# Feed-forward stage: order of PSUM copies around a late narrow product, and two banks for the first narrow products

## The chip, the cores and the metric

The kernel runs on one core of a Trainium2 chip. The metric is device time in microseconds of one execution. Engines: TensorE (PE; its weight loads are PEld), VectorE (DVE), ScalarE (ACT), GpSimd (POOL) and SyncE (SP, which issues the DMAs). PE results land in PSUM, eight banks of 512 fp32 words per partition; ACT and DVE read them from there.

## What is computed

Three layers run one after the other on 4 x 768 tokens (8 heads of 48, so 384 features). Only the last one is touched; the second one hands it its input as a product of two thin matrices.

```
y   = linear_attention(r, k, v, w, u)        # 3072 x 384
c   = softmax(y @ phi, axis=1)               # 3072 x 32
x   = c @ slot_out                           # 3072 x 384, slot_out is 32 x 384
h   = x @ w_in                               # 3072 x 2048
g   = where(h > 0, h, exp(min(h, 0)) - 1)
out = g @ w_out                              # 3072 x 384
```

The weights w_in and w_out arrive as 64-bit floats; the kernel reads them as pairs of 32-bit words and turns them into fp32 itself.

## The kernel before

**The feed-forward by narrow products.** Because x is c @ slot_out, the kernel never forms x. It forms slot_out @ w_in (32 x 2048, the *narrow products*) and then h transposed, block by block, from it and from c transposed. Each fp32 factor of a wide matmul is carried as a rounded part (*high*, written by ACT as fp32r) and the rest (*low*, written by DVE as the difference), side by side in the partitions. So a narrow product must go PE -> PSUM -> ACT `high` -> DVE `low` before a wide matmul can use it as a weight. `through` (L1125) makes the product for 2n columns: two halves `a` of n columns each, the first on partitions 0 to 63 of a PSUM tile `phm`, the second on partitions 64 to 127; the matmuls of the halves alternate over three steps of the contraction. `high` (L1139) and `low` (L1142) round one half into `mst`.

**PSUM.** The pool `fh_p` has two tiles of two banks each, for h (`ph[n]`, "fh" in the profile). The pool `fo_p` has four tiles of one bank, tag `fo`, given out in turn: to the narrow products, and then to the output sums `po[blk, t]`, four for each block of 512 tokens (t = 0 to 3). A tile that is given out again can be written only when the last reader of its previous holder is done.

**Start of the stage.** Columns 0 to 255 (m0) and 256 to 511 (m1) are made first, L1149, each in one `fo` tile, and rounded in the order high(0), low(0), high(1), low(1). Then `hid(0)` (h of the first unit: two matmuls, the first needs half 0 of m0, the second half 1), then the products m3 (columns 1024 to 1279) and m2 (512 to 1023) on PE, while ACT and DVE begin the activation of unit 0 (`tanh`, `expo` on ACT; `neg`, `elu` on DVE; `upper`, the high part of g, on ACT; `lower`, its low part, on DVE). ACT has the roundings of m3 and m2 in between these.

**The main loop.** A unit n is one block of 512 tokens with two tiles of 128 hidden columns; there are 48: first, for each of the six blocks, the five pairs among the first ten column tiles (units 0 to 29; unit n is of block n // 5), then the three pairs of the last six. Step n of the loop issues `hid(n)` on PE; on ACT `leave` (copies of finished sums), `tanh(n)`, `leave`, `expo(n)`, `upper(n-1)`; on DVE `neg(n)`, `lower(n-1)`, `elu(n)`; then, on PE, the output products `outp(n-3, (2, 3))` and `outp(n-2, (0, 1))`, 24 matmuls in all (L1261, L1262, L1264). Steps 6 to 31 without 12 and 22 also carry the widening of late weights (ACT, DVE, POOL, and DMAs on SP), and steps 26, 30 and 33 split late weights (L1286, L1287).

**Sums.** When the fifth pair of a block has been added, the sums of its four `po` tiles are put on the list `done`. `leave(k)` takes k of them off and has ACT copy each to `acc` (L1198). A block's sums 0 and 1 join the list at the end of one step, and 2 and 3 during the next.

**The late product.** At step 22 (`PAUSE[1]`), after `outp(19, (2, 3))`, the kernel makes the narrow product of the columns 1280 to 2047 (`columns(CA, CB // 2)`, "m" below), and rounds it: high(0), low(0), high(1), low(1). The columns are used from unit 30 on. This product takes one `fo` tile between the four of block 3 and the four of block 4. So it takes the bank of block 3's sum 0, and block 4's sums 0, 1, 2 take those of block 3's sums 1, 2, 3, and block 4's sum 3 that of the late product. Block 3's sums 0 and 1 are copied in step 22 itself, its sums 2 and 3 at the top of step 23 on ACT, behind the roundings of the late product. On PE, `outp(20, (0, 1))` of step 22 comes right behind the late product and opens block 4's sums 0 and 1.

```
            if n == PAUSE[1]:
                m = columns(CA, CB // 2)
                for i in range(2):
                    high(*m, i)
                    low(*m, i)
            if n - 2 < N:
                outp(n - 2, (0, 1))
```

The order on each engine is the order of the text; waits between the engines follow from the tiles.

Of the kernel before, what the change touches and what calls it, by code (L numbers as in the profile page):

```python
# [8 lines left out]
F32 = mybir.dt.float32  # L9
# [4 lines left out]
ALU = mybir.AluOpType  # L14
# [222 lines left out]
def kernel(  # L237
# [14 lines left out]
    nc = tc.nc  # L252
# [43 lines left out]
    for a in range(2):  # L296
# [5 lines left out]
        out=mask, in_=mask, compare_op=ALU.is_gt, fill=0.0, base=0, pattern=[[1, 128]], channel_multiplier=-1  # L302
# [94 lines left out]
    with ExitStack() as actx:  # L397
# [333 lines left out]
        def part(j):  # L731
            fs = [[logits], [slots_a], [], [slots_b], [slots_c], [slots_d], [slots_e], [slots_f], []]
            fs = [[(f, j) for f in l] for l in fs]

            def stage(l):
                for f, i in l:
                    f(i)

            return [lambda l=l: stage(l) for l in fs]
# [208 lines left out]
    def half(name, dtype=F32):  # L948
        return ht_p.tile([128, 1024], dtype, tag="ht", name=name)
# [36 lines left out]
    for a in range(2):  # L986
        for q in range(4):
# [3 lines left out]
                out=s3, in_=s3, compare_op=ALU.is_ge, fill=0.0, base=-spe * e, pattern=[[1, NS]],  # L991
# [3 lines left out]
                out=s3, in_=s3, compare_op=ALU.is_ge, fill=0.0, base=spe * e + spe - 1, pattern=[[-1, NS]],  # L995
# [107 lines left out]
    sT = mid.tile([128, KD, 64], F32, name="sT")  # L1103
# [12 lines left out]
    fo_p = main.enter_context(tc.tile_pool(name="fo_p", bufs=4, space=PSUM))  # L1116
# [5 lines left out]

    mst = [half(f"mst{i}", F32R) for i in range(2)]

    def through(c, n, ph):  # L1125
        src, c0 = (win, 0) if c < CA else (win2, CA)
        for kk in range(KD):
            for a in range(2):
                nc.tensor.matmul(
                    out=ph[64 * a:64 * a + 64, :n], lhsT=sT[:, kk, :],  # L1130
                    rhs=src[:, kk, c - c0 + n * a:c - c0 + n * a + n], start=(kk == 0), stop=(kk == KD - 1),
                )
        return ph, c, n

    def halves_of(c, n, a):
        o = mst[c // 1024][:, c % 1024 + n * a:c % 1024 + n * a + n]
        return o[64 * a:64 * a + 64], o[64 - 64 * a:128 - 64 * a]

    def high(ph, c, n, a):  # L1139
        nc.scalar.copy(out=halves_of(c, n, a)[0], in_=ph[64 * a:64 * a + 64, :n])  # L1140

    def low(ph, c, n, a):  # L1142
        hi, lo = halves_of(c, n, a)
        nc.vector.tensor_tensor(out=lo, in0=ph[64 * a:64 * a + 64, :n], in1=hi.bitcast(F32), op=ALU.subtract)  # L1144

    def columns(c, n):
        return through(c, n, fo_p.tile([128, 512], F32, tag="fo", name="phm"))

    m0, m1 = columns(0, 128), columns(256, 128)  # L1149
    for m in (m0, m1):  # L1150
        for i in range(2):
            high(*m, i)
            low(*m, i)
# [19 lines left out]
    def late_wide(j, f):  # L1173
        if 0 <= j < NPB:
            raw, a, dst = pieces[j]
            if f is wide_d:
                f(raw, a, dst)
                del pieces[j]
                if j + 2 < NPB:
                    late_load(j + 2)  # L1180
            else:
                f(raw, a)
# [9 lines left out]
    def leave(n=1):  # L1192
        for _ in range(n):
            if done:
                o, r, second = done.pop(0)
                a = acc[r // 8][:, r % 8, :]
                if not second:
                    nc.scalar.copy(out=a, in_=o)  # L1198
                    continue
                if r < NT // 128 - 4:  # L1200
                    os_ = f2.tile([128, DM], F32, tag="os", name="os", bufs=4)
                    nc.scalar.copy(out=os_, in_=o)  # L1202
                    nc.gpsimd.tensor_tensor(out=a, in0=os_, in1=a, op=ALU.add)  # L1203
                else:
                    nc.vector.tensor_tensor(out=a, in0=o, in1=a, op=ALU.add)
                nc.sync.dma_start(out=out[128 * r:128 * r + 128, :], in_=a)


    ph, th, ex = {}, {}, {}
    NARROW, HALF = 4, 6  # L1210

    def hid(n):
        blk, f = units[n]
        ph[n] = fh_p.tile([128, 2, TB], F32, tag="fh", name="fh")
        for i in range(2):
            nc.tensor.matmul(  # L1216
                out=ph[n][:, i, :], lhsT=mst[(f + i) // 8][:, 128 * ((f + i) % 8):128 * ((f + i) % 8) + 128],
                rhs=cT[:, TB * blk:TB * blk + TB], start=True, stop=True,
            )
        th[n] = f2.tile([128, 2, TB], F32, tag="th", name="th")  # L1220
        ex[n] = f2.tile([128, 2, TB], F32, tag="ex", name="ex")
# [7 lines left out]
    def neg(n, s):  # L1229
        nc.vector.scalar_tensor_tensor(  # L1230
            out=ex[n][:, s], in0=ex[n][:, s], scalar=1.0, in1=th[n][:, s], op0=ALU.add, op1=ALU.mult
        )

    def elu(n, s):
        nc.vector.scalar_tensor_tensor(  # L1235
            out=ex[n][:, s], in0=ex[n][:, s], scalar=0.0, in1=ph[n][:, s], op0=ALU.min, op1=ALU.max
        )
# [7 lines left out]
    def lower(n, s):  # L1245
        nc.vector.tensor_tensor(  # L1246
            out=gl[n][:, s], in0=ex[n][:, s], in1=gh[n][:, s].bitcast(F32), op=ALU.subtract
        )
# [19 lines left out]
    def outp(n, ts):  # L1268
        for t in ts:
            for i in range(2):  # L1270
                term(n, i, t, (0, 1))
        if TB // 128 - 1 in ts:
            gh.pop(n), gl.pop(n)

    def outp_first(n, done=()):
        for x in range(2):
            for i in range(2):
                for t in range(TB // 128):
                    if (i, t, x) not in done:
                        term(n, i, t, (x,))  # L1280
        gh.pop(n), gl.pop(n)

    def late_split(f):
        a, b = (t[:, f % 8:f % 8 + 2, :] for t in whl[f // 8])
        w = wo2[:, f - FA:f - FA + 2, :]
        nc.scalar.copy(out=a, in_=w)  # L1286
        nc.vector.tensor_tensor(out=b, in0=w, in1=a.bitcast(F32), op=ALU.subtract)  # L1287

    def both(f, n, s=slice(0, 2)):
        if 0 <= n < N:  # L1290
            f(n, s)
# [5 lines left out]
    def narrow(n):  # L1297
        u = n - 1
        neg(u, ta)
        lower(u - 1, tb)  # L1300
        elu(u, ta)
        tanh(n, ta)
        upper(u, ta)
        neg(u, tb)
        expo(n, ta)
        lower(u, ta)
        elu(u, tb)
        tanh(n, tb)
        upper(u, tb)
        expo(n, tb)  # L1310
# [7 lines left out]
    tanh(0, ta)  # L1318
    expo(0, ta)
    high(*m3, 0)  # L1320
    tanh(0, tb)
    expo(0, tb)
    high(*m3, 1)
    neg(0, ta)
    elu(0, ta)
# [8 lines left out]
    for i in range(2):  # L1334
        low(*m3, i)
    lower(0, ta)
    elu(0, tb)
    for i in range(2):
        low(*m2, i)
# [8 lines left out]
    for n in range(2, N + 3):  # L1348
        if n < N:
            hid(n)  # L1350
        if n <= NARROW:
            narrow(n)
        else:
            if n == NARROW + 1:
                neg(n - 1, slice(0, 2))
                lower(n - 2, tb)
                elu(n - 1, slice(0, 2))
            leave(1 if done and done[0][1] % 4 == 0 else 2)
            both(tanh, n)
            leave()  # L1360
            both(expo, n)
            both(upper, n - 1)
            j, h = divmod(steps.index(n), 2) if n in steps else (-1, 0)
            if h == 0:
                late_wide(j, wide_a)
            if n in SPLIT:
                late_split(FA + 2 * SPLIT.index(n))
            both(neg, n)
            both(lower, n - 1)
            both(elu, n)  # L1370
            for f in (wide_b3, wide_c, wide_d) if h else (wide_b1, wide_b2):
                late_wide(j, f)
        if n < HALF:
            outp_first(n - 2, early if n == 2 else ())
        else:
            if n > HALF:
                outp(n - 3, (2, 3))
            if n == PAUSE[1]:
                m = columns(CA, CB // 2)
                for i in range(2):  # L1380
                    high(*m, i)
                    low(*m, i)
            if n - 2 < N:
                outp(n - 2, (0, 1))
    leave(4)
# [36 lines left out]
```

## Time and profile before

| | us |
|---|---|
| three runs | 454.84, 455.89, 456.1 |
| median | 455.89 |
| profiled execution, its own time | 454.1 |
| profiled execution, span from first to last instruction | 452.4 |
| PE busy in it | 414.1 (92%) |
| DVE busy in it | 369.3 (82%) |
| ACT busy in it | 262.2 (58%) |
| mean granted TensorE clock | 0.995 |

Times in the rows count from the start of the span. A timeline row has the start, the length, engine, line, operation, and in brackets how long the engine had stood idle before it and what ended that. The length of a matmul runs to its modelled end, so in a stream the matmuls overlap and the distance of their starts is what one costs. The feed-forward stage runs from about 202 us to the end.

### The profile page before, as it was taken

The page shows a single profiled execution, that of the slowest core. Times are in us where ns is not written, and L with a number is a line of the kernel's source. Part 1 is how long each engine was busy: PE and PEld are TensorE (multiplying, and loading weights), DVE is VectorE, ACT ScalarE, POOL GpSimd, SP SyncE. Part 2 cuts the span into 40 slices and gives each one's busy share as a digit, 9 for nine tenths or more (in the row PEclk, how much of TensorE's full clock was granted, in tenths as well). Part 3 has the DMA queues.
Part 4 walks back from the last instruction along what each step waited for, and adds up shares of the span by engine and source line. Part 5 has one row for each costly group of instructions (what it writes and reads, how often), then busy time and mean ns, then how long its engine had stood idle before and what let it go on. Part 6 is the DMA issues. An engine that isn't in the chain of part 4 may idle for free.

```text
span 452.4 us, 10086 instructions
## 1 busy us (share of the span) xinstructions
PE 414.1 (92%) x4021; PEld 361.4 (80%) x4021; DVE 369.3 (82%) x581; ACT 262.2 (58%) x482; POOL 157.2 (35%) x170
## 2 busy tenths in 40 slices
PE   6988988898988989997999999998999899999995
PEld 5876776776776874455999999996989889999994
DVE  5899989899898744768889999995989889768661
ACT  2543453545453332337787878874777768776750
POOL 2355455456446413500003333350213135423340
PEclk9999999999999999999999999998999999999999
DMA  8979799999999968940001111111111002011212
GB/s 124 227 163 268 191 258 265 266 282 186 269 266 260 278 212 280 313 175 1 0 1 35 36 35 38 35 36 35 36 35 35 1 0 72 35 54 52 71 71 76
DMA packets 97575, 57.41 MB, mean 127 GB/s; under 512 B 77808, under 2 KB 89328, under 8 KB 97520
## 3 DMA queue, kind: packets, MB, share of 16 engines
q1 hardware_dynamic: 96704, 56.64, 46.0%
q8 instruction: 33, 0.54, 0.5%
q14 instruction: 22, 0.18, 0.1%
q10 hardware_dynamic: 816, 0.05, 0.1%
HBM read 51.96 MB, written 4.72 MB: 125 GB/s over the span
## 4 chain that ended last, share of the span: by engine, by line
PE 54%; DVE 24%; issue 9%; ACT 7%; DMA 3%; SPq 1%; POOL 1%; DVEq 0%; ACTq 0%; POOLq 0%
PE fo L1261 10%; PE fo L1264 10%; PE fo L1262 10%; DVE ex L1235 4%; DVE ex L1230 4%; PE fh L1216 3%; PE py L612 3%; PE ps_k L522 3%; PE ps_a L554 2%; PE pd L1029 2%; PE ph L1007 2%; DVE am L559 2%; PE py L625 2%; DVE km L517 2%; DVE scr L317 2%
## 5 line engine op out<-in xcount | busy, mean ns | idle before, releaser
L1261 PE MATMUL fo<-wh,gh 128*128 128x384 f32 x384 | 130.8, 341 | 3.8 <-ACT acc L1198 2.7
L1262 PE MATMUL fo<-wl,gh 128*128 128x384 f32 x384 | 130.1, 339 | 0.0
L1264 PE MATMUL fo<-wh,gl 128*128 128x384 f32 x384 | 125.9, 340 | 3.3 <-DVE gl L1246 3.3
L1230 DVE SCALAR_TENSOR_TENSOR ex<-ex,th 128x1024 f32<-128x1024 f32 (+1 forms) x52 | 60.9, 1172 | 23.8 <-ACT ex L1227 23.6
L1261 PEld LDWEIGHTS fo<-wh,gh 128*128 128x128 f32 x384 | 72.5, 189 | 8.6 <-ACT acc L1198 4.3
L1264 PEld LDWEIGHTS fo<-wh,gl 128*128 128x128 f32 x384 | 72.0, 188 | 4.2 <-DVE gl L1246 4.2
L1262 PEld LDWEIGHTS fo<-wl,gh 128*128 128x128 f32 x384 | 72.4, 189 | 1.9
L1224 ACT ACTIVATE th<-fh 128x1024 f32<-128x1024 f32 (+1 forms) x53 | 50.4, 951 | 38.0 <-PE fh L1216 38.0
L1246 DVE TENSOR_TENSOR gl<-ex,gh 128x1024 fp32r<-128x1024 f32 (+1 forms) x52 | 68.3, 1314 | 1.7 <-ACT gh L1243 1.3
L336 POOL TENSOR_TENSOR cv<-raw,cv 128x384 f32<-128x384 f32 x12 | 19.4, 1620 | 136.5 <-ACT gh L1243 51.5
L1235 DVE SCALAR_TENSOR_TENSOR ex<-ex,fh 128x1024 f32<-128x1024 f32 (+1 forms) x52 | 58.8, 1131 | 0.5 <-ACT ex L1227 0.4
L1227 ACT ACTIVATE ex<-fh 128x1024 f32<-128x1024 f32 (+1 forms) x53 | 50.3, 949 | 9.7 <-DVE gl L1246 9.5
L1243 ACT CAST gh<-ex 128x1024 fp32r<-128x1024 f32 (+1 forms) x52 | 51.4, 988 | 6.2 <-DVE ex L1235 4.9
L1203 POOL TENSOR_TENSOR acc<-os,acc 128x384 f32<-128x384 f32 x20 | 26.7, 1346 | 44.0 <-ACT os L1202 44.0
L646 ACT COPY xT<-ps_x 128x384 f32<-128x384 f32 x24 | 11.5, 479 | 43.2 <-PE ps_x L644 43.2
L583 POOL TENSOR_TENSOR qc<-t,w 128x192 f32<-128x192 f32 x20 | 14.5, 725 | 59.7 <-DVE t L582 21.8
L1216 PE MATMUL fh<-cT,mst 128*128 128x512 f32 x96 | 31.1, 404 | 1.9 <-DVE mst L1144 1.1
L559 DVE TENSOR_TENSOR am<-ps_a,mask 128x512 f32<-128x512 f32 x48 | 30.7, 678 | 0.2 <-PE ps_a L554 0.2
L529 DVE TENSOR_TENSOR qd<-rT,ps_k 128x512 f32<-128x512 f32 x24 | 16.5, 686 | 15.3 <-ACT kT L527 15.3
L554 PE MATMUL ps_a<-rT,kT 64*128 64x128 f32 x384 | 27.9, 285 | 0.3 <-ACT kT L527 0.2
L522 PE MATMUL ps_k<-ident,km 128*128 128x128 f32 x96 | 15.6, 285 | 12.4 <-ACT xT L646 6.4
L625 PE MATMUL py<-vd,am 128*64 128x48 f32 x768 | 26.5, 222 | 0.0
(161 smaller groups left out, 695.0 us busy)
## 6 DMA issues: line engine op xcount, KB each, us to landing
we<-in_moe_w_dram SPq DMA_DIRECT2D x14, 768.0 KB, 8.0
we<-in_moe_w_dram SPq DMA_DIRECT2D x16, 512.0 KB, 6.2
rp<-in_r_dram SPq DMA_DIRECT2D x24, 192.0 KB, 4.6
rk<-in_k_dram SPq DMA_DIRECT2D x24, 192.0 KB, 4.6
vd<-in_v_dram SPq DMA_DIRECT2D x24, 192.0 KB, 4.8
out_dram<-acc SPq DMA_DIRECT2D x24, 192.0 KB, 1.9
we<-in_moe_w_dram SPq DMA_DIRECT2D x16, 256.0 KB, 5.4
scr<-in_moe_w_out_dram SPq DMA_DIRECT2D x10, 384.0 KB, 5.7
```

The costliest lines, as they stand in the source:

```text
L554: nc.tensor.matmul(out=aps[a][:, p, :], lhsT=kT[q, p, :], rhs=rT[n][q, p, :], start=True, stop=True)
L559: nc.vector.tensor_tensor(out=am[n, a], in0=aps[a], in1=mask.unsqueeze(1).to_broadcast([128, HP, 128]), op=ALU.mult)
L1216: nc.tensor.matmul(out=ph[n][:, i, :], lhsT=mst[(f + i) // 8][:, 128 * ((f + i) % 8):128 * ((f + i) % 8) + 128], rhs=cT[:, TB * blk:TB * b ...
L1224: nc.scalar.activation(out=th[n][:, s], in_=ph[n][:, s], func=ACTF.Tanh, scale=0.5)
L1227: nc.scalar.activation(out=ex[n][:, s], in_=ph[n][:, s], func=ACTF.Exp)
L1230: nc.vector.scalar_tensor_tensor(out=ex[n][:, s], in0=ex[n][:, s], scalar=1.0, in1=th[n][:, s], op0=ALU.add, op1=ALU.mult)
L1235: nc.vector.scalar_tensor_tensor(out=ex[n][:, s], in0=ex[n][:, s], scalar=0.0, in1=ph[n][:, s], op0=ALU.min, op1=ALU.max)
L1243: nc.scalar.copy(out=gh[n][:, s], in_=ex[n][:, s])
L1246: nc.vector.tensor_tensor(out=gl[n][:, s], in0=ex[n][:, s], in1=gh[n][:, s].bitcast(F32), op=ALU.subtract)
L1261: nc.tensor.matmul(out=o, lhsT=gh[n][:, i, s], rhs=wh, start=(f == first), stop=False)
L1262: nc.tensor.matmul(out=o, lhsT=gh[n][:, i, s], rhs=wl, start=False, stop=False)
L1264: nc.tensor.matmul(out=o, lhsT=gl[n][:, i, s], rhs=wh, start=False, stop=(f == final))
```

## The change

Three things. The first two narrow products get a list of two `fo` tiles each, one for each half (`part` picks the tile). At step 22 `leave(2)` is put in front of the late product. And the late product's two roundings are issued before its two low parts.

```diff
+    def part(ph, n, a):
+        return (ph[a] if isinstance(ph, list) else ph)[64 * a:64 * a + 64, :n]
+
     def through(c, n, ph):
...
-                    out=ph[64 * a:64 * a + 64, :n], lhsT=sT[:, kk, :],
+                    out=part(ph, n, a), lhsT=sT[:, kk, :],
...
     def high(ph, c, n, a):
-        nc.scalar.copy(out=halves_of(c, n, a)[0], in_=ph[64 * a:64 * a + 64, :n])
+        nc.scalar.copy(out=halves_of(c, n, a)[0], in_=part(ph, n, a))
...
-        nc.vector.tensor_tensor(out=lo, in0=ph[64 * a:64 * a + 64, :n], in1=hi.bitcast(F32), op=ALU.subtract)
+        nc.vector.tensor_tensor(out=lo, in0=part(ph, n, a), in1=hi.bitcast(F32), op=ALU.subtract)
...
-    m0, m1 = columns(0, 128), columns(256, 128)
+    m0 = through(0, 128, [fo_p.tile([128, 512], F32, tag="fo", name=f"phm{i}") for i in range(2)])
+    m1 = through(256, 128, [fo_p.tile([128, 512], F32, tag="fo", name=f"phm{i}") for i in range(2)])
...
             if n == PAUSE[1]:
+                leave(2)
                 m = columns(CA, CB // 2)
-                for i in range(2):
-                    high(*m, i)
-                    low(*m, i)
+                for f in (high, low):
+                    for i in range(2):
+                        f(*m, i)
```

## Rows read from the trace of the kernel before

**Rows 1.** Page, busy tenths and granted clock in 40 slices of 11.3 us.

```profile
PE   6988988898988989997999999998999899999995
DVE  5899989899898744768889999995989889768661
PEclk9999999999999999999999999998999999999999
```

**Rows 2.** Windows: us, busy time and count by engine, clock, DMA.

```profile
234.60:281.00 46.40, 45.95 (x255) 44.64 (x254) 44.90 (x50) 36.41 (x48) 15.32 (x8) 1.00 0.12 35
281.00:299.00 18.00, 18.00 (x101) 17.46 (x100) 17.38 (x20) 14.57 (x19) 6.73 (x4) 1.00 0.12 36
308.17:312.00 3.83, 1.63 (x10) 1.00 (x6) 3.26 (x4) 1.46 (x4) 0.00 (x0) 0.94 0.09 35
312.00:316.00 4.00, 3.98 (x14) 3.79 (x15) 0.06 (x1) 1.18 (x2) 0.00 (x0) 0.63 0.00 0
330.00:373.00 43.00, 39.94 (x218) 37.90 (x216) 37.04 (x41) 32.33 (x42) 11.73 (x8) 1.00 0.06 19
373.00:447.00 74.00, 73.50 (x408) 72.02 (x408) 54.44 (x49) 48.77 (x62) 26.68 (x20) 1.00 0.17 60
```

**Rows 3.** Timeline of PE around the late product (L1129) and the first halted sum.

```profile
299.04 0.62 PE L1216 MATMUL fh<-cT,mst 128*128 128x512 f32 x2
303.72 0.62 PE L1216 MATMUL fh<-cT,mst 128*128 128x512 f32 x2
304.18 0.34 PE L1261 MATMUL fo<-wh,gh 128*128 128x384 f32 x1
306.12 0.34 PE L1264 MATMUL fo<-wh,gl 128*128 128x384 f32 x1
306.39 2.16 PE L1129 MATMUL phm<-win,sT 128*64 128x384 f32 x12
308.47 0.44 PE L1261 MATMUL fo<-wh,gh 128*128 128x384 f32 x1
309.46 0.34 PE L1264 MATMUL fo<-wh,gl 128*128 128x384 f32 x1
312.02 0.69 PE L1261 MATMUL fo<-wh,gh 128*128 128x384 f32 x1 [2.23 <-ACT acc L1198]
314.11 1.03 PE L1216 MATMUL fh<-cT,mst 128*128 128x512 f32 x2
319.19 0.63 PE L1216 MATMUL fh<-cT,mst 128*128 128x512 f32 x2
```

**Rows 4.** Timeline of ACT, step 22 and the start of step 23.

```profile
304.38 1.03 ACT L1224 ACTIVATE th<-fh 128x1024 f32<-128x1024 f32 x1 [0.55 <-PE fh L1216]
306.58 1.05 ACT L1243 CAST gh<-ex 128x1024 fp32r<-128x1024 f32 x1
308.62 0.47 ACT L1140 CAST mst<-phm 64x384 fp32r<-64x384 f32 x1 [0.98 <-PE phm L1129]
310.99 0.47 ACT L1140 CAST mst<-phm 64x384 fp32r<-64x384 f32 x1 [1.90 <-DVE mst L1144]
311.49 0.86 ACT L1198 COPY acc<-fo 128x384 f32<-128x384 f32 x2
315.18 1.03 ACT L1224 ACTIVATE th<-fh 128x1024 f32<-128x1024 f32 x1 [2.82 <-PE fh L1216]
```

**Rows 5.** Timeline of DVE over the same steps.

```profile
309.16 1.21 DVE L1235 SCALAR_TENSOR_TENSOR ex<-ex,fh 128x1024 f32<-128x1024 f32 x1
310.41 0.55 DVE L1144 TENSOR_TENSOR mst<-phm,mst 64x384 fp32r<-64x384 f32 x1
317.15 1.23 DVE L1230 SCALAR_TENSOR_TENSOR ex<-ex,th 128x1024 f32<-128x1024 f32 x1 [5.09 <-ACT ex L1227]
```

**Rows 6.** Timeline of the stage's start: roundings, low parts and unit 0.

```profile
202.25 1.53 PE L1129 MATMUL phm<-win,sT 128*64 128x128 f32 x24 [0.32 <-DVE sT L1105]
203.51 0.28 DVE L1144 TENSOR_TENSOR mst<-phm,mst 64x128 fp32r<-64x128 f32 x1 [1.31 <-ACT mst L1140]
203.83 0.55 ACT L1140 CAST mst<-phm 64x128 fp32r<-64x128 f32 x2 [0.35 <-DVE mst L1144]
204.47 0.19 PEld L1216 LDWEIGHTS fh<-cT,mst 128*128 128x128 f32 x1 [0.43 <-DVE mst L1144]
204.77 0.26 ACT L1140 CAST mst<-phm 64x128 fp32r<-64x128 f32 x1 [0.39 <-DVE mst L1144]
204.90 2.17 PE L1129 MATMUL phm<-win,sT 128*64 128x128 f32 x24
205.05 0.60 ACT L1224 ACTIVATE th<-fh 128x512 f32<-128x512 f32 x1
215.71 0.70 PE L1216 MATMUL fh<-cT,mst 128*128 128x512 f32 x2 [0.67 <-DVE ex L1235]
```

**Rows 7.** Other halts of PE in the main loop (timeline of PE).

```profile
238.25 0.44 PE L1261 MATMUL fo<-wh,gh 128*128 128x384 f32 x1 [0.45 <-ACT acc L1198]
337.33 0.44 PE L1264 MATMUL fo<-wh,gl 128*128 128x384 f32 x1 [0.99 <-DVE gl L1246]
357.94 0.44 PE L1264 MATMUL fo<-wh,gl 128*128 128x384 f32 x1 [1.23 <-DVE gl L1246]
```

## What the change should do to the time

> **What bounds the kernel now.** I read the slices first: PE is busy at nine tenths almost throughout from 202 us on, DVE close behind it, and the granted clock shows one slice below nine, the 28th, from 305 to 317 us [rows 1]. Then the windows of the stage: PE has 18.00 us of work in 18.00 us before the late product and 73.50 in 74.00 at the end; between 330 and 373 us it loses some 3 us to DVE, 39.94 of 43.00; and between 308 and 316 us it loses more in 8 us than anywhere else, first standing still (1.63 busy of 3.83), then at a mean clock of 0.63 [rows 2]. So outside a few places the end of the kernel is the start of the stage plus PE's work plus PE's halts, and a halt that goes is worth its length unless something later re-creates it. The change touches the start of the stage and the one long halt. The timelines of these two places carry the rest.
>
> **Part 1, the copies in front of the late product.** PE takes 4.68 us for a unit (hid at 299.04 and 303.72), 0.46 of it for hid (the next matmul starts at 304.18) and 4.22 / 24 = 0.176 for each output matmul [rows 3]. In step 22 it makes the late product from 306.39 to 308.47, adds to block 4's sum 0 until 309.64 (last start 309.46 plus 0.176), and then stands until 312.02, where the wait for ACT's copy L1198 ends [rows 3]. That copy starts at 311.49, right behind the second rounding at 310.99, which itself waited 1.90 us for DVE's first low part; that one could start only at 310.41, when DVE had finished `elu` of 309.16 [rows 4, 5]. So PE waits for a copy whose data have been there since 306.5 (the matmul of 306.12 plus its 0.34 [rows 3]) and which is queued on ACT behind a rounding that waits for DVE.
>
> With the change ACT has the two copies behind `upper` of 306.58, which takes 1.05 us: they start by 307.65 and, at 0.86 for the two, are done by 308.5 [rows 4]. PE wants sum 1's bank at 309.64, so there is 1.1 us to spare. ACT meets the late product at 308.62 as before and rounds both halves by 309.6, before DVE is free at 310.4; DVE's low parts then follow back to back, 310.41 to 311.5 [rows 4, 5]. No transfer moves with the copies: L1198 issues no DMA in the first half of the stage, and no instruction of POOL or SP is passed.
>
> The worth: PE's halt from 309.64 to 312.02 is 2.38 us. The six matmuls of sum 1 then take 312.02 to 314.11, 2.09 us where six in a stream take 6 x 0.176 = 1.06, so 1.03 more; and hid(23) to hid(24) takes 319.19 - 314.11 = 5.08 us in place of 4.68, 0.40 more [rows 3]. The last two are the clock: granted at 0.63 on average between 312 and 316 us, after the halt, which is a part at the lower level of 1.2 GHz [rows 2]. A halt of 1.23 us later on is in a window whose clock is 1.00 [rows 2, 7], so the fall goes with the long halt, and I count it as removed. Sum 2.38 + 1.03 + 0.40 = 3.8 us. Bounds: 2.4 if the clock still falls; 3.9 if the slower first matmul after the product goes too.
>
> What is late next? hid(23) comes at 309.64 + 1.06 = 310.7, tanh(23) 0.66 later at 311.4 (303.72 to 304.38 in step 22), where ACT is free since 309.6 [rows 3, 4]. Then `expo`, and DVE's `neg(23)` two ACT instructions after tanh, 1.97 us as from 315.18 to 317.15, so at 313.3 [rows 4, 5]. DVE is free at 311.5: of its idle 5.09 us about 1.8 remain, so it is not behind and step 23 starts for PE, ACT and DVE in the same relation as before, only 3.8 us earlier. Block 4's sum 3 takes the late product's bank: PE wants it after hid(23) (0.46) and six matmuls, at 310.7 + 0.46 + 1.06 = 312.2, and DVE has read it at 311.5; 0.7 us to spare.
>
> Everything after is tied to step 23 by waits among the same engines, the halts for DVE between 330 and 373 us too; these should come 3.8 us earlier and be as long.
>
> **Part 2, two banks for the first products.** Now the second rounding on ACT starts at 203.83, 0.04 us after the first low part on DVE ends (203.51 + 0.28), having idled 0.35; the fourth again idles 0.39 for the third low part; and tanh(0) starts at 205.05, right behind that fourth rounding of 204.77 + 0.26 [rows 6]. ACT and DVE so alternate on one tile, though they read different partitions. With a bank for each half, the second rounding follows the first at about 203.5 and the second low part the first at 203.8, done by 204.1; it was done at 204.4, as the weight load at 204.47 waits for it. That load, for hid(0)'s second matmul, moves to about 204.1, so 0.35 us. The rounding of m1 starts when m1 is made (202.25 + 1.53 = 203.8) and its second half ends near 204.35, so tanh(0) is no longer held by it. If tanh needs only hid's first matmul it comes 0.65 us earlier, if it needs both 0.35 earlier. The next thing on ACT, the rounding of m3, needs the product started at 204.90, which moves by 0.35 to 0.4 behind hid(0) [rows 6]. I take 0.4, between 0.35 and 0.6. From there to 215.71, where PE's next unit still waits 0.67 for DVE, the chain runs through ACT and DVE without a gap that would swallow it [rows 6]; behind that PE's stream carries it to the end.
>
> The rule that speaks against this part is in the Trainium skill, "PSUM — Partial Sum Buffer", section "PSUM bank collisions raise a hardware error": engines may be in different quadrants (32 partitions) of one bank at once, and guards need to be only by bank and quadrant. By it the two halves need no wait for each other, a second bank brings nothing, and the sum would be part 1's 3.8 us, 452.1. The trace differs: the wait at 203.83 is there, though the halves share no partition, so the guard is coarser than that.
>
> Unseen: alternating banks within the 24 matmuls of m0 and m1. They take 1.53 us; if they no longer overlapped they could take at most twice that, and if nothing changes, none. hid writes its two banks in turn at full pace in the stream [rows 3], the nearest row, so I take none. The third and fourth `fo` tiles are needed 2.6 us earlier than before (202.25 in place of 204.90); their former holders belong to the earlier stage, whose last PSUM tile is read by the copies for which the products wait in any case (the 0.32 us at 202.25) [rows 6]. The products m3 and m2 now take m0's two banks, which must be read by both engines; hid(0), ahead of them on PE, waits for the same low parts, so nothing is added.
>
> **Sum.** 3.8 + 0.4 = 4.2 us. The span of 452.4 becomes 448.2 and that execution's 454.1 becomes 449.9. It lies 1.8 us under the median of the runs, 455.89, so against the median the forecast is 451.7.
>
> **Rivals.** (a) *The second bank lifts no wait* (the guard is not by tile): only 3.8, 452.1. For it: two reads of different partitions wait today, which shows that the guard is not fine. Against: ACT's first rounding of m1, another tile, follows without a wait (two in 0.55 at 203.83) [rows 6]. (b) *The halt shrinks but the clock still falls, or a shorter wait replaces it*: block 4's sum 3 has 0.7 us to spare, and DVE that is 1.5 us later than worked out would halt PE there for 0.8; or the clock costs its 1.4. Gain 2.8 to 3.4 with part 2, 452.5 to 453.1. (c) *The gain is given back*: between 330 and 373 us PE waits for DVE; if what DVE does there were tied to something that does not move, a DMA or POOL, PE would meet it 3.8 us sooner and wait that much longer. Only part 2's 0.4 or nothing is left, 455.5. Against: DVE's 5.09 us idle before step 23 are themselves the halt's doing [rows 5], and the DMAs use 6 to 17% [rows 2]. (d) *Slower*: without the halt PE runs on from its wait at 238.25 to the first one for DVE, now at 337.33 and then near 333.5: some 95 us, where the unbroken stretches are now 71 us (238.25 to 309.64) and, in the last window, 74 us, both at clock 1.00 but for their ends [rows 2, 3, 7]. If the granted clock fell to the lower level somewhere past 74 us of unbroken work, each microsecond of work there would cost one more. From 4.2 us at that level on the gain is eaten; at 8 us of such work the time is 455.9 - 4.2 + 8 = 459.7. Nothing in the rows hints at it: the only fall comes after standing still.
>
> **Chances and range.** Forecast 0.64; (a) 0.14; (b) 0.11; (c) 0.08; (d) 0.03. Faster by over 0.3% (1.4 us, about what a measurement of this kernel can tell from no change) covers the first three, 0.89; same 0.08; slower 0.03. The three runs spread from 1.05 us below the median to 0.2 above, and the profiled one lies 1.8 below; so the range goes from 449.8 (full gain on an execution like the profiled one) to 453.2, the lower gain of (b).
>
> **What would show it.** Right: in the timeline of PE no idle row between the late product and hid(23); the two L1198 rows before the late product's first rounding, both roundings before the first low part; the 28th slice of the clock back at nine; `neg(23)` with an idle time near 1.8 us in place of 5.09; tanh(0) 0.35 to 0.6 us earlier than now against the start of the first product, and PE's unit at 215.71 near 215.3. Wrong: a wait of PE for DVE's `mst` at block 4's sum 3; a second rounding that still waits for the first low part at 203.8; longer waits for `gl` between 330 and 373 us; a clock below 1.00 past 310 us.

## The result, and the profile after

| | before | changed |
|---|---|---|
| median, us | 455.37 (454.11 to 456.31, 6 runs) | 450.0 (449.89 to 450.5, 6 runs) |
| profiled execution | 454.1 | 449.94 |
| its span | 452.4 | 448.2 |
| its mean clock | 0.995 | 0.997 |

The ratio is 0.9887, 95% interval 0.9867 to 0.9907: faster by about 5 us. On the profiled executions, on which the sum was made, it is 4.2 us. Executions of one kernel differ here in their mean granted clock: of the kernel before, beside the runs for the experiments, two took 452.82 and 452.86 at 0.999, many 454.1 at 0.992 to 0.996, and several 456 at 0.985. So medians of few runs move by a microsecond or more, and the traces decide what follows.

The page of the changed kernel, slices of busy tenths and granted clock; the 28th slice of the clock, 8 before, is a 9 now, as all are but the last, in which PE ends its work:

```profile
PE   6988989898888898997999999999999899999995
PEclk9999999999999999999999999999999999999998
```

Windows of the changed kernel (span, then busy time of PE, PEld, DVE, ACT and POOL with counts, then clock and DMA). Where PE had 1.63 of 3.83 us and then a clock of 0.63 [rows 2], it is busy all the time at 1.00:

```profile
304.00:312.00 8.00, 8.00 (x46) 6.33 (x45) 7.04 (x9) 5.98 (x10) 1.66 (x1) 1.00 0.15 49
312.00:326.00 14.00, 14.00 (x79) 13.73 (x78) 12.77 (x13) 9.71 (x12) 2.93 (x2) 1.00 0.09 29
326.00:369.00 43.00, 39.69 (x217) 37.68 (x215) 37.04 (x42) 32.11 (x42) 11.71 (x8) 1.00 0.06 19
```

The timeline of PE in the changed kernel (lines are three or four higher than before: L1220 is hid, L1265 the first output matmul, L1132 the narrow products):

```profile
303.28 0.63 PE L1220 MATMUL fh<-cT,mst 128*128 128x512 f32 x2
305.96 2.16 PE L1132 MATMUL phm<-win,sT 128*64 128x384 f32 x12
308.05 0.45 PE L1265 MATMUL fo<-wh,gh 128*128 128x384 f32 x1
310.26 0.64 PE L1220 MATMUL fh<-cT,mst 128*128 128x512 f32 x2
314.96 0.63 PE L1220 MATMUL fh<-cT,mst 128*128 128x512 f32 x2
...
333.10 0.44 PE L1268 MATMUL fo<-wh,gl 128*128 128x384 f32 x1 [0.99 <-DVE gl L1250]
...
353.70 0.44 PE L1268 MATMUL fo<-wh,gl 128*128 128x384 f32 x1 [1.23 <-DVE gl L1250]
```

From hid(22) to hid(24) PE now takes 314.96 - 303.28 = 11.68 us, before 319.19 - 303.72 = 15.47 [rows 3]: 3.79 us gone. The two halts for DVE come at the same distance as before and are as long, 0.99 and 1.23 [rows 7].

ACT of the changed kernel in step 22 and at the start of step 23. The two copies (L1202) stand ahead of the roundings (L1143), and those follow each other without a wait [rows 4]:

```profile
306.15 1.05 ACT L1247 CAST gh<-ex 128x1024 fp32r<-128x1024 f32 x1
307.08 0.88 ACT L1202 COPY acc<-fo 128x384 f32<-128x384 f32 x2
308.19 0.96 ACT L1143 CAST mst<-phm 64x384 fp32r<-64x384 f32 x2 [0.23 <-PE phm L1132]
310.93 1.03 ACT L1228 ACTIVATE th<-fh 128x1024 f32<-128x1024 f32 x1 [1.79 <-PE fh L1220]
```

DVE of the changed kernel: the low parts in one go, and 1.80 us of idle time ahead of `neg(23)` in place of 5.09 [rows 5]:

```profile
309.99 1.12 DVE L1147 TENSOR_TENSOR mst<-phm,mst 64x384 fp32r<-64x384 f32 x2
312.91 1.22 DVE L1234 SCALAR_TENSOR_TENSOR ex<-ex,th 128x1024 f32<-128x1024 f32 x1 [1.80 <-ACT ex L1231]
```

The start of the stage in the changed kernel [rows 6]. Four roundings run in a row, and four low parts; hid's two matmuls follow from 203.78 and end at 204.61; `tanh(0)` starts at 204.65:

```profile
202.20 1.53 PE L1132 MATMUL phm<-win,sT 128*64 128x128 f32 x24 [0.32 <-DVE sT L1105]
203.15 1.16 ACT L1143 CAST mst<-phm 64x128 fp32r<-64x128 f32 x4 [1.79 <-PE phm L1132]
203.44 1.25 DVE L1147 TENSOR_TENSOR mst<-phm,mst 64x128 fp32r<-64x128 f32 x4 [1.30 <-ACT mst L1143]
203.78 0.83 PE L1220 MATMUL fh<-cT,mst 128*128 128x512 f32 x2
204.65 0.60 ACT L1228 ACTIVATE th<-fh 128x512 f32<-128x512 f32 x1 [0.34 <-PE fh L1220]
215.31 0.70 PE L1220 MATMUL fh<-cT,mst 128*128 128x512 f32 x2 [0.67 <-DVE ex L1239]
```

From the first product to `tanh(0)` it is 2.45 us, before 2.80, and to the unit at 215.31 it is 13.11, before 13.46: 0.35 us gone. The other 0.05 of the 4.2 lies ahead of the stage, which begins at 202.20 in place of 202.25, in code that the change leaves alone; it is scatter between executions.

### The profile page after: what moved, and what is told of

It reads as the page before. It is cut to its first block, busy times and chain, and to the rows that moved or that the text cites. A ratio compares the mean times of both kernels' runs of the same rounds, so it can differ in the third digit from the quotient of the medians.

```text
span 448.2 us, 10085 instructions
## 1 busy us (share of the span) xinstructions
PE 412.9 (92%) x4021; PEld 360.7 (80%) x4021; DVE 369.3 (82%) x581; ACT 262.1 (58%) x482; POOL 157.0 (35%) x170
## 4 chain that ended last, share of the span: by engine, by line
PE 64%; DVE 18%; ACT 7%; issue 6%; DMA 4%; SPq 1%; DVEq 0%; ACTq 0%
PE fo L1265 12%; PE fo L1268 12%; PE fo L1266 12%; PE fh L1220 4%; PE ps_a L554 3%; PE py L612 3%; PE py L625 3%; PE ps_k L522 3%; DVE ex L1234 2%; DMA we<-in_moe_w_dram 2%; DVE ex L1239 2%; PE pd L1029 2%; PE ph L1007 2%; DVE am L559 2%; PE pu L541 1%
## 5 line engine op out<-in xcount | busy, mean ns | idle before, releaser
L1265 PE MATMUL fo<-wh,gh 128*128 128x384 f32 x384 | 130.2, 339 | 1.5 <-ACT gh L1247 1.0
L1265 PEld LDWEIGHTS fo<-wh,gh 128*128 128x128 f32 x384 | 72.1, 188 | 5.9 <-ACT acc L1202 2.4
L1220 PE MATMUL fh<-cT,mst 128*128 128x512 f32 x96 | 30.5, 399 | 1.8 <-DVE mst L1147 1.1
L601 POOL TENSOR_TENSOR bv<-vd,bs 128x384 f32<-128x384 f32 x24 | 20.3, 846 | 17.8 <-ACT bs L596 17.6
```

Of the source, the lines that this page charges most:

```text
L1220: nc.tensor.matmul(out=ph[n][:, i, :], lhsT=mst[(f + i) // 8][:, 128 * ((f + i) % 8):128 * ((f + i) % 8) + 128], rhs=cT[:, TB * blk:TB * b ...
L1265: nc.tensor.matmul(out=o, lhsT=gh[n][:, i, s], rhs=wh, start=(f == first), stop=False)
```

## Experiments

The theory: 3.8 us come from step 22, where the copies no longer queue behind a rounding that waits for DVE, and where the clock no longer falls behind the halt; 0.35 us come from the start, where two banks lift a wait. The rivals: the bank lifts nothing; the clock falls for another reason; the gain is given back to DVE later; unbroken work lets the clock fall.

**Each part alone: the two banks.**

```diff
 # against the changed kernel
-                leave(2)
                 m = columns(CA, CB // 2)
-                for f in (high, low):
-                    for i in range(2):
-                        f(*m, i)
+                for i in range(2):
+                    high(*m, i)
+                    low(*m, i)
```

> The kernel before with two PSUM tiles each for the first two narrow products, step 22 left as it was. Theory (the gain is 3.8 us from step 22 and 0.35 to 0.4 us from the start of the stage, and they add): 0.35 to 0.4 us under the kernel before, tanh(0) some 2.45 us after the first product's start in place of 2.80; PE still stands for 2.2 us behind the late product and its clock falls after it. Rival (the second bank lifts no wait, all 4.2 us are step 22's): 0 us, the second rounding waits for the first low part. Rival (the two parts interact, the earlier start is what lets the halt go): over 1 us, halt shorter than 2 us.

Measured: 453.94 us against 454.19, ratio 0.9996 (0.9976 to 1.0017), so 0.35 us can't be told on the wall. The timeline of this kernel:

```profile
203.62 1.53 PE L1132 MATMUL phm<-win,sT 128*64 128x128 f32 x24 [0.32 <-DVE sT L1105]
206.06 0.60 ACT L1228 ACTIVATE th<-fh 128x512 f32<-128x512 f32 x1 [0.33 <-PE fh L1220]
313.65 0.44 PE L1265 MATMUL fo<-wh,gh 128*128 128x384 f32 x1 [2.25 <-ACT acc L1202]
```

From product to `tanh(0)` 2.44 us, as in the changed kernel, so the bank lifts the wait; the halt of PE is there with its 2.25 us, so the early start has no part in its going. The two parts are independent.

**The copies alone.**

```diff
 # against the kernel before
             if n == PAUSE[1]:
+                leave(2)
                 m = columns(CA, CB // 2)
```

> The kernel before with leave(2) in front of the late product and nothing else: one bank for each first product, and the late product still rounded high, low, high, low. Theory: the copies alone free the banks in time, no halt of PE and no fall of the clock, 3.7 to 3.8 us under the kernel before; the second rounding still waits for the first low part (about 1.9 us on ACT), and that costs at most 0.1 us, because tanh(23) comes at about the time at which it ends. Rival (the order of the roundings is needed too, tanh(23) queues behind the second rounding or block 4's sum 3 waits for the last low part): a new wait of 0.3 to 1 us on ACT or PE, 2.8 to 3.5 us under the kernel before.

Measured: 450.37 us against 454.19, ratio 0.9915 (0.9889 to 0.9941), about 3.9 us; span 448.4. Timeline of ACT:

```profile
307.46 0.88 ACT L1198 COPY acc<-fo 128x384 f32<-128x384 f32 x2
308.56 0.47 ACT L1140 CAST mst<-phm 64x384 fp32r<-64x384 f32 x1 [0.22 <-PE phm L1129]
310.94 0.48 ACT L1140 CAST mst<-phm 64x384 fp32r<-64x384 f32 x1 [1.90 <-DVE mst L1144]
311.44 1.03 ACT L1224 ACTIVATE th<-fh 128x1024 f32<-128x1024 f32 x1
```

The second rounding still waits 1.90 us, at almost no cost: `tanh(23)` starts right behind it, 7.77 us behind hid(22) in place of the 7.65 of the whole change, and PE does not feel these 0.12 us. hid(22) to hid(24) takes 11.66 us (303.67 to 315.33), what it takes with all of the change. The copies are the whole gain of step 22.

**The order of the roundings alone.**

```diff
 # against the kernel before
-                for i in range(2):
-                    high(*m, i)
-                    low(*m, i)
+                for f in (high, low):
+                    for i in range(2):
+                        f(*m, i)
```

> The kernel before with both roundings of the late product in front of its low parts and nothing else; the copies stay behind the roundings. Theory (PE waits for the copy, and the copy for the second rounding's wait for DVE): the roundings end near 309.5 us, the copy of block 3's sum 2 near 310.0, PE wants its bank at 309.64, so a halt of 0.3 to 0.4 us is left of 2.38, and no fall of the clock: 3.4 us under the kernel before. Rival (the clock falls because of the late product's 64-column matmuls and any halt behind them): the halt is 0.4 us but the clock still falls, 1.9 to 2.0 us under the kernel before.

Measured: 450.99 us, ratio 0.9929 (0.9903 to 0.9956), about 3.2 us. The timeline of this kernel, then a window:

```profile
309.58 0.86 ACT L1198 COPY acc<-fo 128x384 f32<-128x384 f32 x2
310.12 0.45 PE L1261 MATMUL fo<-wh,gh 128*128 128x384 f32 x1 [0.34 <-ACT acc L1198]
```

```profile
312.00:316.00 4.00, 4.00 (x25) 4.00 (x24) 2.08 (x2) 2.82 (x3) 0.00 (x0) 1.00 0.00 0
```

The halt is 0.34 us, and the clock stays at 1.00 behind the same late product, so in these profiles the fall goes with the long halt and not with the product. hid(22) to hid(24) takes 12.26 us, 0.6 more than without a halt. So a halt costs more than the idle time in its row. That time counts from the modelled end of the last matmul, 0.34 us behind its start, while in a stream the next one starts after 0.176: this is 0.16. And the first matmul behind the halt takes 0.28 us to the next start in place of 0.176: this is 0.10. So either half of step 22's edit does most of the work, and the two don't add.

**One bank, but the roundings first, at the start.**

```diff
 # against the changed kernel
-    m0 = through(0, 128, [fo_p.tile([128, 512], F32, tag="fo", name=f"phm{i}") for i in range(2)])
-    m1 = through(256, 128, [fo_p.tile([128, 512], F32, tag="fo", name=f"phm{i}") for i in range(2)])
+    m0, m1 = columns(0, 128), columns(256, 128)
     for m in (m0, m1):
-        for i in range(2):
-            high(*m, i)
-            low(*m, i)
+        for f in (high, low):
+            for i in range(2):
+                f(*m, i)
```

> The changed kernel with one PSUM tile for each of the first two narrow products again, but there, too, both roundings in front of the low parts. Theory (the wait is per tile, so within one tile the first low part waits for the second rounding): hid(0)'s first matmul about 0.25 us later than in the changed kernel, its second about 0.2 later, tanh(0) 0.2 later: 4.0 us under the kernel before, 0.2 over the changed one, which is too little for the clock on the wall but visible in the trace from the first product's start to tanh(0) (2.45 us in the changed kernel, 2.65 here). Rival (only the alternation costs, the bank itself nothing): 2.45 us here too.

Measured: 450.76 us, ratio 0.9915 (0.9888 to 0.9941). Its timeline:

```profile
202.30 1.53 PE L1132 MATMUL phm<-win,sT 128*64 128x128 f32 x24 [0.32 <-DVE sT L1105]
203.83 1.25 DVE L1147 TENSOR_TENSOR mst<-phm,mst 64x128 fp32r<-64x128 f32 x4 [1.58 <-ACT mst L1143]
204.17 0.89 PE L1219 MATMUL fh<-cT,mst 128*128 128x512 f32 x2 [0.34 <-DVE mst L1147]
205.10 0.60 ACT L1227 ACTIVATE th<-fh 128x512 f32<-128x512 f32 x1 [0.69 <-PE fh L1219]
```

2.80 us from product to `tanh(0)`, not the 2.65 expected: exactly what the kernel before takes. The first low part now waits for the second rounding, hid's first matmul is late, and so its second is. Where PE needs the halves one after the other, reordering within one tile only moves the wait; the second bank is needed. Whether the wait goes by tile or by bank these runs don't separate, since each of these tiles is a bank.

**The halt made longer.**

```diff
 # against the kernel before, behind the late product's roundings
+                high(*m, 1)
+                high(*m, 1)
```

> The kernel before with the second rounding of the late product issued three times in place of once (the same values again), so that ACT reaches the copies about 0.95 us later and PE stands behind the late product for 3.2 us in place of 2.2. Theory (what PE loses here is the halt plus a stretch at the lower clock whose length does not grow with the halt): 0.95 us over the kernel before, hid(22) to hid(24) 16.4 us in place of 15.5. Rival (the clock's cost grows with the halt): 1.3 to 1.6 us over. Rival (the halt is covered by slack later): 0 us. Besides: where the fall of the clock follows the halt only in some executions, the longer halt should make it follow in all, and the spread of the runs shrink.

Measured: 455.99 us against 454.63, ratio 1.0035 (1.002 to 1.005), so 0.9 to 2.3 us more. Its timeline of PE, then a window:

```profile
303.62 0.63 PE L1216 MATMUL fh<-cT,mst 128*128 128x512 f32 x2
313.04 0.69 PE L1261 MATMUL fo<-wh,gh 128*128 128x384 f32 x1 [3.34 <-ACT mst L1140]
315.13 1.05 PE L1216 MATMUL fh<-cT,mst 128*128 128x512 f32 x2
321.26 0.62 PE L1216 MATMUL fh<-cT,mst 128*128 128x512 f32 x2
```

```profile
312.00:318.00 6.00, 4.96 (x15) 4.76 (x16) 0.00 (x0) 3.58 (x6) 0.00 (x0) 0.50 0.00 0
```

The halt is 1.11 us longer, 3.34 in place of 2.23, but hid(22) to hid(24) grows by 2.17, to 17.64: hid(23) to hid(24) now takes 6.13 us in place of 5.08 [rows 3], because the clock stays at half, 1.2 GHz, until past 318 us. The theory's 0.95 us is too little for this execution; the rival, that the clock's cost grows too, fits it. It is not so in all: the fastest of the twelve took 455.04 at a clock of 0.995, 0.94 over the 454.1 that is commonest for the kernel before. The spread of the twelve, 455.04 to 457.66, is not clearly smaller than that of the seventeen of the kernel before, 452.82 to 455.87; none of the twelve has a clock above 0.996. A small part of the loss comes back in the same execution: the first halt for DVE is 0.74 us there in place of 0.99 [rows 7], as in the profile of the banks alone (0.76). How long the clock stays down thus differs between executions, and these runs don't settle what decides it. The row's releaser is a rounding and not a copy; the slip of the reading, further down, says why.

**The halts behind the late product, and a kernel faster than both.** Between 326 and 369 us PE of the changed kernel stands 3.3 us in three halts for DVE, whose subtraction in the late split of the weights stands 1.9 us waiting for ACT's copy, ahead of all else that DVE has to do. The lines are hid(27) and hid(28), the third halt, and the first subtraction; the first two halts are shown above.

```profile
329.02 0.62 PE L1220 MATMUL fh<-cT,mst 128*128 128x512 f32 x2
334.96 0.63 PE L1220 MATMUL fh<-cT,mst 128*128 128x512 f32 x2
369.09 0.44 PE L1268 MATMUL fo<-wh,gl 128*128 128x384 f32 x1 [1.07 <-DVE gl L1250]
```

```profile
329.62 1.15 DVE L1291 TENSOR_TENSOR wl<-wo,wh 128x768 fp32r<-128x768 f32 x1 [1.94 <-ACT wh L1290]
```

Put behind `elu`, the subtraction finds the copy ready.

```diff
 # against the changed kernel; late_split(f, 0) is the copy on ACT, late_split(f, 1) the subtraction on DVE
             if n in SPLIT:
-                late_split(FA + 2 * SPLIT.index(n))
+                late_split(FA + 2 * SPLIT.index(n), 0)
             both(neg, n)
             both(lower, n - 1)
             both(elu, n)
+            if n in SPLIT:
+                late_split(FA + 2 * SPLIT.index(n), 1)
```

> The changed kernel with the late split of weights (steps 26, 30, 33) cut in two: the copy on ACT stays, the subtraction on DVE goes behind elu(n) in place of in front of neg(n), so DVE no longer stands 1.9 us for ACT's copy. Theory (the end is the stage's start plus PE's work plus PE's halts, so each halt that goes is worth its length): the three halts of PE behind the late product, 0.99, 1.23 and 1.07 us, go, 3.3 us under the changed kernel, 446.7. PE then runs without a halt over 0.3 us from 238 us to its end near 439 us, some 200 us. Rival (such an unbroken stretch lets the granted clock fall): a clock below 1.00 somewhere past 330 us and less than 2.5 us gained, or a loss. Rival (the gain is given back: DVE is the bound there and its work stays the same): 0 to 1.5 us gained.

Measured: 446.58 us (446.57 to 448.48), ratio to the kernel before 0.9839 (0.9815 to 0.9863); span 444.9, 3.3 us under the changed kernel's. Windows, then, from the timeline of PE, the only halt over 0.3 us between 240 us and the end, with the hid before and behind it:

```profile
238.00:330.00 92.00, 92.00 (x509) 88.44 (x510) 87.94 (x94) 71.10 (x93) 30.83 (x18) 1.00 0.11 35
330.00:365.00 35.00, 34.87 (x194) 33.68 (x192) 34.79 (x38) 29.06 (x37) 13.08 (x7) 1.00 0.08 23
366.00:440.00 74.00, 73.27 (x409) 71.79 (x407) 51.78 (x47) 46.58 (x60) 26.48 (x20) 1.00 0.17 61
```

```profile
361.97 0.62 PE L1220 MATMUL fh<-cT,mst 128*128 128x512 f32 x2
365.58 0.44 PE L1266 MATMUL fo<-wl,gh 128*128 128x384 f32 x1 [0.71 <-DVE wl L1291]
367.63 0.62 PE L1220 MATMUL fh<-cT,mst 128*128 128x512 f32 x2
```

PE works for over 125 us with no halt of note, and at clock 1.00 to its end, so unbroken work of this length does not bring the clock down here: the rival of the prediction on the slow side falls, as the changed kernel's 95 us from 237.85 to 333.10 had already shown.

The three halts are gone, but a new one of 0.71 us has come: the last of the three moved subtractions ends too late, and now PE waits for its result (`wl`, L1291) itself. That the gain is the sum of the three idle times, 3.3 us, is therefore luck. The units around the old halts took 5.94 (329.02 to 334.96), 6.18 and 6.04 us in place of 4.69, so they cost 4.1 us and not 3.3; the unit of the new halt takes 5.66 (361.97 to 367.63), so 1.0 is lost again. The rest is the unit behind the first halt, 5.05 us before and 4.69 now. A halt of PE that goes is worth its idle time and some 0.26 us more, as with the 0.34 us above.

**A halt at the start filled.**

```diff
 # against the kernel of the run before this one, in term(), ahead of a sum's first product
+            if n == 0 and i == 0 and t < 3:
+                for _ in range(2):
+                    nc.tensor.matmul(out=o, lhsT=gh[n][:, i, s], rhs=wh, start=True, stop=True)
```

> The kernel of e6_split_late with six more matmuls for PE where it stands for 1.08 us in front of hid(2): the first product of unit 0's sums 0, 1 and 2 is issued twice more ahead of itself, each one overwritten by the next, so the sums are the same. Theory (the falls of the clock near 211 us that some executions show follow the two halts of about 1 us there): that halt shrinks to about 0.1 us, the fastest time is that of e6_split_late within 0.3 us, 446.6 to 446.9, and no execution has a fall near 211 us, so all lie within 0.5 us of the fastest. Rival (that fall follows the first of the two halts, at 208 us, or something ahead of the stage): the same spread as before, 1 to 2 us, in about one execution of three. Rival (the six matmuls are on the path of hid(2)): 0.2 to 0.5 us slower throughout.

Measured: 446.58 us again (446.51 to 447.76), ratio 0.9817 (0.979 to 0.9844). The six matmuls cost nothing, and the halt in front of hid(2) is gone: its row has no wait.

```profile
211.98 0.74 PE L1220 MATMUL fh<-cT,mst 128*128 128x512 f32 x2
```

Of five executions four lie within 0.21 us; the fifth, at 447.76, is the profiled one and had its fall of the clock elsewhere, ahead of the stage, as this window shows (1.00 in the profile of the run before this one); the stage begins at 203.45 in place of 202.23:

```profile
100.00:150.00 50.00, 43.22 (x708) 35.47 (x706) 44.53 (x90) 23.80 (x71) 24.88 (x27) 0.97 0.96 241
```

That the clock can fall at the start of this stage is seen in the profiles of the banks alone (0.53 from 212 to 214 us) and of the start with one bank (0.50 there); whether filling the halt cures that, five runs with none can't show.

## Why the prediction came out right

*Part 1, 3.8 us*: 3.79 measured. The sum's three pieces were the halt, slower matmuls and a slow unit behind it; all went together, as the order alone shows for the clock (1.00 behind a halt of 0.34). What is late next was placed right: `tanh(23)` 7.65 us behind hid(22), worked out as 7.7, and `neg(23)` with 1.80 us of idle time, worked out as 1.8. Of the two edits in step 22 the prediction told only that PE waits for a copy behind a rounding behind DVE; the experiments add that the copies alone give it all, and the order alone most of it.

*Part 2, 0.4 us*: 0.35 measured, the lower bound. `tanh(0)` needs both of hid's matmuls, though it reads the first one's bank alone (it starts 0.04 after the second ends), so the case "only the first" does not hold. The wait between the halves was real, though they share no partition, and a tile for each half lifted it, so rival (a) falls. The rule that the prediction set against this part, from the Trainium skill, "PSUM — Partial Sum Buffer", section "PSUM bank collisions raise a hardware error", says what must be kept apart; the same section calls a guard by bank alone the simple version, and the wait seen here fits that one.

*The cover*: DVE was not behind, block 4's sum 3 found its bank free (PE has no idle row from hid(22) to hid(24)), the halts between 330 and 373 us kept their length, and nothing was given back.

*The base*: here the forecast was off. The sum on the profiled execution gave 449.9, and 449.94 was measured; the step that put it on the median, 455.89 - 4.2 = 451.7, came out 1.7 us above the measured 450.0. So the gain on the medians was 5.4 us where 4.2 were forecast, and the result lies only 0.2 us above the low end of the range, 449.8, which was set for executions like the profiled one. The base was a median of three runs, two of them at 456. Their clocks are not on record; most other executions of the kernel before near 456 have 0.985 or 0.986, against 0.995 in the execution whose rows were summed, so the clock had probably fallen for longer in them. The runs of the changed kernel lie close together, 449.89 to 450.5. That the change takes away one cause of falls may be a reason for it, but it is not shown: kernels with the same step 22 spread further, to 451.56 (one bank at the start) and, from 446.57, to 448.48 (the late split moved).

*A slip of the reading*: the `fo` tiles are not given out strictly in turn. The bank numbers in the built programs fit a pool that gives out next the tile released first. In the kernel before, block 4's sums 0 to 3 take the banks of block 3's sums 1 and 2, of the late product, and of block 3's sum 3; in the changed kernel the late product's bank goes to sum 3, as the prediction had it. With the longer halt it goes to sum 1, which is why PE waits for a rounding there. The wait that mattered, sum 1 for the copy of block 3's sum 2, was the one named.

## What to carry to other kernels

When PE halts for a PSUM bank, look at what stands ahead of the releasing copy in its engine's queue: a copy whose data have long been there belongs in front of any instruction that may wait for another engine. The same holds for the subtraction on DVE: an instruction that waits for another engine goes behind the work that doesn't. Here that took away the long halt with the clock behind it, and three halts later on. But look also at who needs the result of what is moved back: in the last of the three places PE then waited for it. A halt's worth is read from the starts of the units around it, since the idle time of its row leaves out some 0.26 us here. A gain worked out on one execution should be set against that execution, since the median may stand on others.

## What the runs showed that was not expected

The granted clock fell to half with the halts of 2.2 and 3.3 us in the profiles, for about 3.4 us (from 311.6 to 315.0 in the kernel before) and 6.8 us (from 311.5 to 318.3 with the longer halt), but not behind those of 0.34 to 1.23 us in the main loop; near 212 us, behind two halts of about 1 us, it fell in two profiles and not in the others. Nor does the fall come at a fixed place. In the kernel before it comes within the halt, which ends at 312.02; with the banks alone the halt is as long and ends at 313.65, and the fall comes behind it, past 314 us. A window of each, the kernel before first:

```profile
311.00:312.00 1.00, 0.00 (x0) 0.00 (x0) 0.50 (x1) 0.98 (x3) 0.00 (x0) 0.78 0.00 0
314.00:315.00 1.00, 1.00 (x6) 1.00 (x5) 0.00 (x0) 0.00 (x0) 0.00 (x0) 0.77 0.00 0
```

Two executions of the kernel before took 452.82 and 452.86 us at a mean clock of 0.999, 1.3 us under its commonest time, which is about the 1.4 us that the sum gave to the clock; they have no trace, so that the halt was there without the fall is likely but not shown. A halt's length alone thus does not decide, in these runs, whether or when the clock falls; what else does stays open.
